# Fixed rounds over the experts, weights read where they stand, and a run-time rest

## The chip, the cores and the metric

The kernel runs on one core of one Trainium2 chip. The metric is the device time of one execution in microseconds (us), the median of several runs. TensorE (PE) multiplies, VectorE (DVE) and ScalarE (ACT) work element by element, GpSimd (POOL) issues the scatters, and SyncE (SP) issues loads, transposing DMAs and gathers. Each engine takes its own instructions in order.

## The reference

A gated linear scan over 4 sequences of 5056 tokens with 256 channels, then a mixture of 8 experts, where each of the 20224 tokens goes to the one expert with the largest logit:

```python
f = lower_bound + (1 - lower_bound) * sigmoid(f_logit); i = 1 - f
h = f[:, t] * h + i[:, t] * x[:, t]; y[:, t] = h          # for each t
logits = y @ w_gate; e_idx = argmax(logits)                # w_gate 256 x 8
gate_w = softmax(logits)[e_idx]; eom = sigmoid(y @ w_output_gate)
for e in range(8):                                         # w1 256 x 1024, w2 1024 x 256
    out[mask] = gate_w * eom[:, e] * (relu(y[mask] @ w1[e]) @ w2[e])
```

How many tokens an expert gets is known only when the kernel runs.

## The kernel before

**Chunks.** The scan and the gating run over 40 chunks of 512 tokens (`chunk`, L240). A chunk is a row of 17 stages, one per `yield` without a kind: stage 0 is a tanh on ACT (L251), 1 a product on DVE (L255), 3 the scan on DVE (L266), 5 a small matmul (L277), 6 a few small DVE instructions, 7 and 8 the high part (ACT, L296) and the low part (DVE, L300) of the rows, 10 the gating matmuls (L311, L316), 12 and 15 small DVE instructions, 16 four scatters (L413) of the rows to the region of their expert in `scr`. SP turns the rows by transposing DMAs in stages 8 and 10 (L293). In stage 4 a chunk issues the load of the next (L236, L237), into one of two buffers (`XB`).

**The order of the work.** `pump` runs one stage of each chunk under way beside the tasks of the experts; every `PERIOD` (8) pumps one more chunk begins. Up to a cut (the end of the weights' preparation) a scheduler orders the engines' instructions; behind it each engine takes them as the code makes them.

**Early tiles.** The weights are loaded and split into two float16 parts (`w1s`, `w2s`) in the first part of the run. Beside that, two rounds of 128 rows of each expert (`EARLY`, planned after chunks 3 and 5) are computed with the weights read where they stand (`first1`, `first2`).

**Run-time tiles.** All further work is done in tiles of 256 rows of one expert, which expert being a number that DVE computed (`plan`, some 24 small instructions for each two tiles) and that is loaded into a register (`expert`, L622). [...] `gemm1` (L655 to L657) makes four pieces `ph` of 2 x 256 columns, ACT takes the relu (L659), DVE its low part (`low`, L667), and `gemm2` (L685 to L687) follows one tile behind; then ACT scales (L728) and POOL scatters to the output (L732). There are 64 such tiles (`sure`: what any routing fills).

**The rest.** What is left is done in tiles of 128 rows, again with copies. Of these 18 are always run. Their true number, `count`, is loaded at the end, and two `tc.If` blocks (3 more tiles from 18, 16 more from 21) run where it is larger (L942 to L951).

Of the kernel before, what the change touches and what calls it, by code (L numbers as in the profile page):

```python
# [27 lines left out]
PERIOD = 8  # L28
PUMPS = 2.25
FILL = 12  # L30
MORE = (18, 21)
EARLY = (3, 5)
# [8 lines left out]
LEAD = 2  # L41
PLAN = 4
# [8 lines left out]
def tile_scan_moe(  # L51
# [32 lines left out]
    def sure(tokens):  # L84
        """tiles of 256 tokens of one expert that any routing of so many tokens fills beside the first tiles"""
        return max(0, -(-(tokens - len(EARLY) * E * P - E * 255) // 256))

# [7 lines left out]
    scr = dp.tile([E * R + P, RW], I16, name="scr")  # L95

# [16 lines left out]
    nc.gpsimd.iota(jcol, pattern=[[0, 1]], base=0, channel_multiplier=1, allow_small_or_imprecise_dtypes=True)  # L113
    eye = cp.tile([P, E], F32, name="eye")
# [19 lines left out]
    def pow2(ss, t, nm):  # L134
        """from a norm's square: s, a power of two with s times the norm below 2 ** t, and 2 / s"""
# [58 lines left out]
    # writes to rows of their own need no order among them; a reader waits for those it reads  # L194
# [12 lines left out]
    # rows behind each expert's rows: factor 0, an index no scatter takes  # L207
# [3 lines left out]
    fresh.append(nc.sync.dma_start(out=scr[FREE : FREE + P, :], in_=padt))  # L211
    apart(fresh[0], "scr")
    row2 = [cp.tile([P, NB, RW], I16, name=f"rows{i}") for i in range(2)]
    # the places of the last experts' weights serve the first chunks until then
# [25 lines left out]
    def chunk(c):  # L240
        """the steps of a chunk; each takes from the steps before what other engines made there"""
# [185 lines left out]
    firsts = []  # L427

    def plan_first():
        """for each expert: its next 128 rows, or the free rows behind all regions where it has fewer yet"""  # L430
# [8 lines left out]
        nc.vector.tensor_scalar(n, n, float(P), None, ALU.is_ge)  # L439
# [4 lines left out]
        nc.vector.scalar_tensor_tensor(out=dn, in0=n, scalar=float(P), in1=done, op0=ALU.mult, op1=ALU.add)  # L444
        yield SMALL
        nc.vector.scalar_tensor_tensor(out=m, in0=m, scalar=float(FREE), in1=eye, op0=ALU.add, op1=ALU.mult)
        tab = sp.tile([P, 2], I32, tag="pf_tab", name="pf_tab", bufs=len(EARLY))
# [6 lines left out]
        firsts.append([(tab, e, 1, new) for e in range(E)])  # L454

    def plan(k, nb, last):
# [27 lines left out]
        sel = t8("sel")  # L484
        yield SMALL
        nc.vector.tensor_scalar(sel, cum, jcol, None, ALU.is_gt)
        yield SMALL
        nc.vector.scalar_tensor_tensor(out=sel, in0=cex, scalar=jcol, in1=sel, op0=ALU.is_le, op1=ALU.mult)
        r = t8("r")
        yield SMALL  # L490
        nc.vector.tensor_scalar(r, cex, jcol, -float(unit), ALU.subtract, ALU.mult)
        yield SMALL
        nc.vector.scalar_tensor_tensor(out=r, in0=done, scalar=1.0, in1=r, op0=ALU.mult, op1=ALU.add)
        yield SMALL
        nc.vector.tensor_tensor(out=r, in0=r, in1=boff, op=ALU.add)
        yield SMALL
        nc.vector.tensor_tensor(out=r, in0=r, in1=sel, op=ALU.mult)
        if last:
            # slots past the last tile take the rows behind expert 0's
# [3 lines left out]
            idle = t8("idle")  # L503
            yield SMALL
            nc.vector.tensor_scalar(idle[:, 0:1], cum[:, E - 1 : E], jcol, cnt[:, 0:1], ALU.is_le, ALU.mult)
            yield SMALL
            nc.vector.tensor_tensor(out=r[:, 0:1], in0=r[:, 0:1], in1=idle[:, 0:1], op=ALU.add)
            prog["count"] = sp.tile([P, 1], I32, tag="pl_count", name="pl_count", bufs=1)
# [6 lines left out]
        tab = sp.tile([P, 2], I32, tag="pl_tab", name="pl_tab", bufs=8)  # L515
        new = list(fresh)
        fresh.clear()
        for j in range(k):
            slots.append((tab, j, nb, new))
        yield SMALL  # L520
        with nc.allow_low_precision("whole numbers"):
            nc.vector.tensor_reduce(out=tab[:, 0:1], in_=r, axis=AX.X, op=ALU.add)
        yield SMALL
        nc.vector.tensor_tensor(out=sel, in0=sel, in1=eidx, op=ALU.mult)
        yield SMALL
        with nc.allow_low_precision("whole numbers"):
            nc.vector.tensor_reduce(out=tab[:, 1:2], in_=sel, axis=AX.X, op=ALU.add)
# [74 lines left out]
    mpool = {}  # L602

    def gather(t, slot, e=None):
        tab, j, nb, new = slot
        n = nb * P
        r = nc.sync.value_load(tab[j : j + 1, 0:1], min_val=0, max_val=FREE + P - n)
        xq = gp.tile([P, 2, KD, 256], I16, tag="xq", name="xq")
        mt = gp.tile([P, 2, 4], I16, tag="mt", name="mt", bufs=4)
# [8 lines left out]
        return dict(xh=xq[:, 0].bitcast(F16), xl=xq[:, 1].bitcast(F16), mt=mt, nb=nb, tab=tab, j=j, id=t, ev=e)  # L618
# [5 lines left out]
    def factors(T):  # L624
        nb, ev = T["nb"], T["ev"]
        col = cinv[:, ev : ev + 1] if isinstance(ev, int) else cinv[:, ds(ev, 1)]
        fac = sp.tile([P, 2], F32, tag="fac", name="fac", bufs=4)
# [17 lines left out]

    def gemm1(T, q):
        mp, n = mpool["m"], T["nb"] * P
        ph = pp.tile([P, 2, 256], F32, tag="h", name="ph", bufs=4)
        w = T[f"w1_{q // 2}"]
        for i in range(2):  # L650
            f = (2 * q + i) % 4
            for k in range(KD):
                first, last = k == 0, k == KD - 1
                o = ph[:, i, 0:n]
                nc.tensor.matmul(out=o, lhsT=w[:, f, k, 0, :], rhs=T["xh"][:, k, 0:n], start=first, stop=False)  # L655
                nc.tensor.matmul(out=o, lhsT=w[:, f, k, 0, :], rhs=T["xl"][:, k, 0:n], start=False, stop=False)  # L656
                nc.tensor.matmul(out=o, lhsT=w[:, f, k, 1, :], rhs=T["xh"][:, k, 0:n], start=False, stop=last)  # L657
        hh = mp.tile([P, 2, 256], F16, tag="hh", name="hh", bufs=6)
        nc.scalar.activation(hh[:, :, 0:n], ph[:, :, 0:n], AF.Relu)  # L659
        T[f"h{q}"] = (ph, hh)  # L660

    def low(T, q):
        n = T["nb"] * P
        ph, hh = T[f"h{q}"]
        hl = mpool["m"].tile([P, 2, 256], F16, tag="hl", name="hl", bufs=6)
        yield BIG
        nc.vector.scalar_tensor_tensor(  # L667
            out=hl[:, :, 0:n], in0=ph[:, :, 0:n], scalar=0.0, in1=hh[:, :, 0:n], op0=ALU.max, op1=ALU.subtract
        )
        T[f"h{q}"] = (hh, hl)  # L670

    def gemm2(T, q):
        nb = T["nb"]
        if q == 0:
            T["y"] = pp.tile([P, 2, D], F32, tag="y", name="py", bufs=2)
        y, w = T["y"], T[f"w2_{q // 2}"]
        hh, hl = T.pop(f"h{q}")
        for i in range(2):
            f = (2 * q + i) % 4
            for b in range(nb):  # L680
                first = q == 0 and i == 0 and b == 0
                last = q == 3 and i == 1
                c = slice(b * P, (b + 1) * P)
                o = y[:, b, :]
                nc.tensor.matmul(out=o, lhsT=hh[:, i, c], rhs=w[:, f, 0, :], start=first, stop=False, skip_group_check=True)  # L685
                nc.tensor.matmul(out=o, lhsT=hh[:, i, c], rhs=w[:, f, 1, :], start=False, stop=False, skip_group_check=True)  # L686
                nc.tensor.matmul(out=o, lhsT=hl[:, i, c], rhs=w[:, f, 0, :], start=False, stop=last, skip_group_check=True)  # L687

    # the first tile of an expert: its weights are read where they stand
# [31 lines left out]
    def evacuate(T):  # L721
        nb = T["nb"]
        if isinstance(T["ev"], int):
# [15 lines left out]
    prog = {"begun": 0, "tick": 0, "done": 0, "left": 0.0, "planned": 0, "final": False, "got": 0, "rounds": 0}  # L739
    live = []  # L740
    total = sure(N)
    tail = (N - 256 * total + E * (P - 1)) // P
    ntile = total + tail

    planning = []

    def loading(c):
        """the steps of chunk c, with the load of the next once the chunk before has freed its place"""
# [241 lines left out]
```

## Time and profile before

| | |
|---|---|
| device time, 3 runs | 1030.67 us median, 1029.03 to 1031.43 |
| span of the profiled execution | 1016.9 us, which is 13.8 us below that median |
| PE, DVE, ACT, POOL busy | 911.9, 887.5, 511.4, 376.5 us |
| weight copies on DVE | 164 of `w1s` (115.1 us), 164 of `w2s` (111.8 us) |
| first run-time tile begins, last matmul | 183.2 us, 1000.26 us |

The page gives the profiled execution's span, from its first to its last instruction; its device time isn't listed apart, and the 13.8 us stand for what lies around the span. Busy time is the union of an engine's instructions. A busy PE is not PE at its peak, since matmuls are pipelined and overlap in the records: the start of one to the start of the next tells the rate.

### The profile page before, as it was taken

How to read it: one execution, taken by the hardware profiler on the slowest of the kernel's cores; microseconds unless marked ns; L12 is line 12 of the kernel's file. 1: busy time of each engine (PE TensorE's matmuls, PEld its weight loads, DVE VectorE, ACT ScalarE, POOL GpSimd, SP SyncE). 2: the span in 40 equal slices, each digit the busy share in tenths (PEclk: the TensorE clock that was granted, in tenths of full speed). 3: DMA queues.
4: the chain of work that ended last, by engine and by line, in shares of the span. 5: the costliest groups of instructions: out<-in, count | busy, mean ns of one | idle time of the engine just before them, and what ended most of it. 6: DMA issues, size and time to landing. Idle time of an engine off the chain costs nothing.

```text
span 1016.9 us, 27437 instructions
## 1 busy us (share of the span) xinstructions
PE 911.9 (90%) x9775; PEld 822.8 (81%) x9775; DVE 887.5 (87%) x2803; ACT 511.4 (50%) x1075; POOL 376.5 (37%) x378
## 2 busy tenths in 40 slices
PE   2268998899999999999999999999999999999993
PEld 2157887788888888888888888888888888899993
DVE  7989896899999999999999999999999998758781
ACT  5667774545545555455455554454455543333331
POOL 1523234343444444433444434344444344221221
PEclk9999999999999999999999999999999999999997
DMA  8899966755566565555565565555665534312120
GB/s 309 202 308 287 267 153 154 179 137 138 138 141 151 135 149 153 137 138 137 137 149 141 157 145 132 139 135 132 149 144 152 138 85 104 95 49 45 47 55 16
DMA packets 238547, 146.34 MB, mean 144 GB/s; under 512 B 202558, under 2 KB 204224, under 8 KB 238401
## 3 DMA queue, kind: packets, MB, share of 16 engines
q1 hardware_dynamic: 222752, 101.74, 43.2%
q0 software_dynamic: 15360, 42.74, 13.7%
q8 instruction: 80, 1.31, 0.6%
q14 instruction: 67, 0.54, 0.2%
q10 hardware_dynamic: 288, 0.02, 0.0%
HBM read 58.38 MB, written 44.49 MB: 101 GB/s over the span
## 4 chain that ended last, share of the span: by engine, by line
DVE 54%; issue 17%; DMA 11%; PE 10%; POOL 3%; ACT 2%; SPq 1%; DVEq 1%; POOLq 0%; ACTq 0%
DVE hl L667 11%; DVE xt L266 7%; DVE w L637 5%; DMA rows<-ft 5%; DVE w L643 4%; DVE xt L255 4%; DVE ft L300 3%; POOL out_dram L732 2%; PE ph L655 1%; PE ph L657 1%; PE ph L656 1%; DMA xq<-scr 1%; PE py L685 1%; PE py L687 1%; PE py L686 1%
## 5 line engine op out<-in xcount | busy, mean ns | idle before, releaser
L655 PE MATMUL ph<-xq,w 128*128 128x256 f16 (+1 forms) x1312 | 331.0, 261 | 0.3 <-DVE xv L142 0.3
L657 PE MATMUL ph<-xq,w 128*128 128x256 f16 (+1 forms) x1312 | 331.2, 261 | 0.0
L656 PE MATMUL ph<-xq,w 128*128 128x256 f16 (+1 forms) x1312 | 331.1, 261 | 0.0
L685 PE MATMUL py<-w,hh 128*128 128x256 f16 x1168 | 318.6, 273 | 0.5 <-ACT ft L296 0.3
L687 PE MATMUL py<-w,hl 128*128 128x256 f16 x1168 | 318.6, 273 | 0.0
L686 PE MATMUL py<-w,hh 128*128 128x256 f16 x1168 | 318.5, 273 | 0.0
L732 POOL DMA_INDIRECT out_dram<-yo,mt x146 | 167.9, 1150 | 298.8 <-ACT yo L728 275.1
L413 POOL DMA_INDIRECT scr<-rows,dst x154 | 175.4, 1139 | 229.3 <-issue 215.5
L659 ACT ACTIVATE hh<-ph 128x512 f16<-128x512 f32 (+1 forms) x328 | 178.7, 545 | 153.1 <-PE ph L657 152.8
L667 DVE SCALAR_TENSOR_TENSOR hl<-ph,hh 128x512 f16<-128x512 f32 (+1 forms) x328 | 204.6, 624 | 10.9 <-ACT hh L659 9.1
L655 PEld LDWEIGHTS <-w 128*128 128x128 f16 x1312 | 128.0, 98 | 12.4 <-DVE w L637 0.6
L637 DVE COPY w<-w1s 128x2048 f16 x164 | 115.1, 702 | 26.1 <-PE ph L657 24.7
L657 PEld LDWEIGHTS <-w 128*128 128x128 f16 x1312 | 128.1, 98 | 11.7
L656 PEld LDWEIGHTS <-w 128*128 128x128 f16 x1312 | 128.1, 98 | 11.4
L687 PEld LDWEIGHTS <-hl 128*128 128x128 f16 x1168 | 114.2, 98 | 13.2
L686 PEld LDWEIGHTS <-hh 128*128 128x128 f16 x1168 | 114.2, 98 | 13.2 <-issue 0.8
L685 PEld LDWEIGHTS <-hh 128*128 128x128 f16 x1168 | 114.2, 98 | 12.5
L643 DVE COPY w<-w2s 128x2048 f16 x164 | 111.8, 682 | 0.5 <-PE py L687 0.3
L260 ACT ACTIVATE ft<-ft,fb,fa 128x512 f32<-128x512 f32 (+1 forms) x76 | 60.6, 807 | 100.7 <-DVE xt L255 98.0
L296 ACT ACTIVATE ft<-xt,sa 128x512 f16<-128x512 f32 (+1 forms) x76 | 50.2, 708 | 106.1 <-DVE li L285 101.9
L266 DVE TENSOR_TENSOR_SCAN xt<-ft,xt 128x512 f32<-128x512 f32 (+4 forms) x78 | 90.7, 1170 | 0.0
L728 ACT ACTIVATE yo<-py,fac 128x256 f32<-128x256 f32 x146 | 61.6, 465 | 26.4 <-PE py L687 25.7
(178 smaller groups left out, 1311.5 us busy)
## 6 DMA issues: line engine op xcount, KB each, us to landing
ft<-in_fT_dram SPq DMA_DIRECT2D x37, 512.0 KB
xt<-in_xT_dram SPq DMA_DIRECT2D x37, 512.0 KB
w<-in_wT_dram SPq DMA_DIRECT2D x32, 512.0 KB
scr<-rows,dst POOLq DMA_INDIRECT x154, 3.3
rows<-ft SPq DMA_TRANSPOSE x152
out_dram<-yo,mt POOLq DMA_INDIRECT x146, 2.8
xq<-scr SPq DMA_TRANSPOSE x99
scr<-padt SPq DMA_DIRECT2D x9, 136.0 KB
```

Source lines behind the costliest of these rows:

```text
L266: nc.vector.tensor_tensor_scan(out=xt[:, k, a:z], data0=ft[:, k, a:z], data1=xt[:, k, a:z], initial=init, op0=ALU.mult, op1=ALU.add)
L413: ins = nc.gpsimd.indirect_dma_start(out=scr[:, :], out_offset=IOA(ap=dst[:, b : b + 1], axis=0), in_=rows[:, b, :], in_offset=None)
L637: nc.vector.tensor_copy(out=w, in_=w1f[:, ds(T["ev"] * (2 * WH) + h * 2 * QH, 2 * QH)])
L655: nc.tensor.matmul(out=o, lhsT=w[:, f, k, 0, :], rhs=T["xh"][:, k, 0:n], start=first, stop=False)
L656: nc.tensor.matmul(out=o, lhsT=w[:, f, k, 0, :], rhs=T["xl"][:, k, 0:n], start=False, stop=False)
L657: nc.tensor.matmul(out=o, lhsT=w[:, f, k, 1, :], rhs=T["xh"][:, k, 0:n], start=False, stop=last)
L659: nc.scalar.activation(hh[:, :, 0:n], ph[:, :, 0:n], AF.Relu)
L667: nc.vector.scalar_tensor_tensor(out=hl[:, :, 0:n], in0=ph[:, :, 0:n], scalar=0.0, in1=hh[:, :, 0:n], op0=ALU.max, op1=ALU.subtract)
L685: nc.tensor.matmul(out=o, lhsT=hh[:, i, c], rhs=w[:, f, 0, :], start=first, stop=False, skip_group_check=True)
L686: nc.tensor.matmul(out=o, lhsT=hh[:, i, c], rhs=w[:, f, 1, :], start=False, stop=False, skip_group_check=True)
L687: nc.tensor.matmul(out=o, lhsT=hl[:, i, c], rhs=w[:, f, 0, :], start=False, stop=last, skip_group_check=True)
L732: ins = nc.gpsimd.indirect_dma_start(out=out[:, :], out_offset=IOA(ap=T["mt"][:, b, 2:4].bitcast(I32), axis=0), in_=T["yo"][:, b, :], in_o ...
```

## The change

Eleven rounds with fixed experts take the place of the two early rounds and of most run-time tiles: six rounds of 128 rows of each expert and five of 256, each planned after a given chunk (`ROUNDS`). In a round every expert has its turn in fixed order, so the weights are read in place, without copies. An expert that does not yet have a full 128 or 256 rows when its round is planned gets a block of padding rows instead (`FREE`), and its rows stay for later (`plan_round`; the block is computed all the same). The first two rounds (`FIRST`) are computed early as before. What the fixed rounds leave is done with run-time tiles and copies: 8 tiles of 256 rows and then tiles of 128, of which again 18 are always run; if `count` is over 18, one block of 19 more is run, and within it, if it is over 37, one of 112 more. A chunk begins every 6 pumps instead of every 8. The work of the tiles is one row of pieces of 512 columns: a tile of 128 rows has two of them (before: four of 256), the second matmuls follow `LAG` (4) pieces behind, and the gathers are issued two tiles ahead instead of one.

```diff
-PERIOD = 8
+PERIOD = 6
-MORE = (18, 21)
-EARLY = (3, 5)
+MORE = (18, 37)
+ROUNDS = (
+    (1, 3), (1, 5), (1, 8), (1, 10), (1, 13), (1, 15),
+    (2, 19), (2, 23), (2, 28), (2, 33), (2, 37),
+)
+FIRST = 2
+LAG = 4
...
+    rows_round = sum(nb for nb, _ in ROUNDS) * P
+    total = max(0, -(-(N - E * rows_round - E * 255) // 256))
+    tail = (N - 256 * total + E * (P - 1)) // P
...
-        nc.vector.tensor_scalar(n, n, float(P), None, ALU.is_ge)
+        nc.vector.tensor_scalar(n, n, float(unit), None, ALU.is_ge)
...
+    def weights1(T, f):
+        return w1s[:, T["ev"], f] if T["fixed"] else T[f"w1_{f // 4}"][:, f % 4]
...
     def gemm1(T, q):
+        n, nf = T["nb"] * P, 4 // T["nb"]
+        ph = pp.tile([P, 512], F32, tag="h", name="ph", bufs=4)
+        for i in range(nf):
+            w, o = weights1(T, nf * q + i), piece(ph, T)[:, i, :]
...
+    fixed += [(r, e) for r in range(len(ROUNDS)) for e in range(turns[r] if r < FIRST else 0, E)]
+    ntile = len(fixed) + total + tail
...
+        for s in range(end + LAG + 2):
+            T, q = flat[s] if s < end else (None, 0)
+            U, u = flat[s - LAG] if LAG <= s < end + LAG else (None, 0)
+            if T is not None and q == 0 and T + 2 < t1 + more:
+                ahead(T + 2)
...
+            step(RATE, tasks)
...
+    base = len(fixed) + total
+    experts(0, base + cuts[0], 0)
...
+    def rest_of(i):
+        if i + 1 < len(cuts):
+            with tc.If(used > cuts[i]):
+                experts(base + cuts[i], base + cuts[i + 1], 0)
+                ordered(0, 0)
+                rest_of(i + 1)
```

On DVE, in the middle of the run. `hl` is the low part of a piece, `ft<-xt` (L300, now L307) and `xt<-ft` (L255, now L262; L266 the scan) are a chunk's, `w` the copied weights, `fac` the tile's factors. Before:

```order
L300 SCALAR_TENSOR_TENSOR ft<-xt,sa,ft 128x512
L629 ISA
L629 TENSOR_SCALAR fac<-mt,cinv 128x2
L255 SCALAR_TENSOR_TENSOR xt<-ft,xt 128x512
L643 ISA
L643 COPY w_0_8969<-w2s 128x2048
L667 SCALAR_TENSOR_TENSOR hl<-ph,hh 128x512
L255 SCALAR_TENSOR_TENSOR xt<-ft,xt 128x512
L637 ISA
L637 COPY w_1_9038<-w1s 128x2048
L667 SCALAR_TENSOR_TENSOR hl<-ph,hh 128x512
```

and now, at the same kind of place:

```order
L642 TENSOR_SCALAR fac<-mt,cinv 128x2
L262 SCALAR_TENSOR_TENSOR xt<-ft,xt 128x512
L687 SCALAR_TENSOR_TENSOR hl<-ph,hh 128x512
L262 SCALAR_TENSOR_TENSOR xt<-ft,xt 128x512
L307 SCALAR_TENSOR_TENSOR ft<-xt,sa,ft 128x512
L687 SCALAR_TENSOR_TENSOR hl<-ph,hh 128x512
L307 SCALAR_TENSOR_TENSOR ft<-xt,sa,ft 128x512
```

The copies are gone from between the low parts; two chunks' large instructions stand closer together.

On PE, at the end of what is always run, before (`L947` loads the count, `L949` is the branch):

```order
L687 LDWEIGHTS hl
L687 MATMUL py<-w_1_19982,hl 128x256
L947 TENSOR_LOAD pl_count
L949 COMPARE_AND_BRANCH
L655 LDWEIGHTS w_0_20034
L655 MATMUL ph<-xq,w_0_20034 128x128
```

and now (`L992` and `L986`):

```order
L704 LDWEIGHTS hl
L704 MATMUL py<-w_1_19072,hl 128x256
L992 TENSOR_LOAD pl_count
L986 COMPARE_AND_BRANCH
L676 LDWEIGHTS w_0_19174
L676 MATMUL ph<-xq,w_0_19174 128x128
```

The form is the same; what stands behind the first branch is now a block of 19 tiles (2736 instructions of PE, a load of weights and a matmul for each of 1368) instead of 3, and the second branch stands inside that block instead of behind it.

On SP, in the middle of the run, before, from a chunk's second pair of transposes (`rows<-ft`) to the next tile's gather (`xq`, `mt`):

```order
L293 DMA_TRANSPOSE rows_133<-ft 128x4x128 x2
L236 DMA ft<-in_fT_dram 128x2x512
L237 DMA xt<-in_xT_dram 128x2x512
L607 TENSOR_LOAD pl_tab
L607 ISA x2
L610 ISA
L610 DMA_TRANSPOSE xq<-scr 128x4x256
```

and now:

```order
L300 DMA_TRANSPOSE rows_136<-ft 128x4x128 x2
L243 DMA ft<-in_fT_dram 128x2x512
L244 DMA xt<-in_xT_dram 128x2x512
L620 TENSOR_LOAD tabs
L620 ISA x2
L623 ISA
L623 DMA_TRANSPOSE xq<-scr 128x4x128
```

The order is the same, but the next chunk begins two pumps after its load is issued, where it was four.

More of the change, by code (lines that the diff above doesn't have):

```diff
@@ L425, in tile_scan_moe, with plan_round @@
     slots = []
-    firsts = []
-    def plan_first():
+    rounds = []
+    tabs = cp.tile([P, 2 * len(ROUNDS)], I32, name="tabs")
+    def plan_round(nb):
+        unit = nb * P
         done = sched["done"]
@@ L453, in plan_first @@
         fresh.clear()
-        firsts.append([(tab, e, 1, new) for e in range(E)])
+        rounds.append([(tab, e, nb, new) for e in range(E)])
     def plan(k, nb, last):
@@ L502, in plan @@
             nc.vector.tensor_copy(out=ends, in_=cnt)
-            idle = t8("idle")
+            prog["count"] = sp.tile([P, 1], I32, tag="pl_count", name="pl_count", bufs=1)
             yield SMALL
[L505 to L508, printed above, removed]
             nc.vector.tensor_copy(out=prog["count"], in_=cum[:, E - 1 : E])
@@ L670, in low @@
         T[f"h{q}"] = (hh, hl)
     def gemm2(T, q):
-        nb = T["nb"]
+        nb, nf = T["nb"], 4 // T["nb"]
         if q == 0:
             T["y"] = pp.tile([P, 2, D], F32, tag="y", name="py", bufs=2)
[L676 to L679, printed above, removed]
-            for b in range(nb):
[L681 to L687, printed above, removed]
+        y = T["y"]
@@ L792, in step, with slot @@
             prog["left"] -= 1.0
-            pump(tasks, need)
+            pump(tasks)
             tasks = []
+    fixed = []
     tiles = {}
+    def slot(t):
+        if t < len(fixed):
+            r, e = fixed[t]
+            return (rounds[r][e], e) if r < len(rounds) else None
+        return (slots[t - len(fixed)], None) if t - len(fixed) < len(slots) else None
     def ahead(t):
-        while len(slots) <= t and len(slots) < ntile:
-            plans(1)
+        while not slot(t):
+            plans()
             if planning:
@@ L853, in tile_scan_moe @@
     deep = WPB // 2
-    for n in range(min(EARLY[0], NCH)):
+    for n in range(PRE):
         load_chunk(n)
@@ new lines, in experts, with later @@
+        nbs = [(2 if t - len(fixed) < total else 1) if t >= len(fixed) else ROUNDS[fixed[t][0]][0] for t in range(t0, t1)]
+        flat, begin, at = [], {}, {}
+        for t, nb in zip(range(t0, t1), nbs):
+            begin[t] = len(flat)
+            flat += [(t, q) for q in range(2 * nb)]
+        end = len(flat)
+        def later(s, act):
+            at.setdefault(s, []).append(act)
+        last = {}
+        for t, nb in zip(range(t0, t1), nbs):
+            if t < len(fixed):
+                continue
+            for fetch, h, lag in ((fetch1, 0, 0), (fetch1, 1, 0), (fetch2, 0, LAG), (fetch2, 1, LAG)):
+                use = begin[t] + h * nb + lag
+                s = last[fetch, h] + 1 if (fetch, h) in last else max(use - 2, 0)
+                assert s <= use
+                last[fetch, h] = use + nb - 1
+                later(s, (fetch, t, h))
@@ new lines, in experts @@
+        ahead(t0)
+        ahead(t0 + 1) if t0 + 1 < t1 else None
+        done = []
+        for s in range(end + LAG + 2):
+            tasks = []
+            T, q = flat[s] if s < end else (None, 0)
+            U, u = flat[s - LAG] if LAG <= s < end + LAG else (None, 0)
+            if T is not None and q == 0 and T + 2 < t1 + more:
+                ahead(T + 2)
+            for fetch, t, h in at.get(s, []):
+                X = tiles[t]
+                if X["ev"] is None:
+                    alone(expert(X))
+                tasks.append(fetch(X, h))
+            if U is not None and u == 0:
+                tasks.append(factors(tiles[U]))
+            if 1 <= s <= end:
+                t, p = flat[s - 1]
+                tasks.append(low(tiles[t], p))
+            step(RATE, tasks)
+            for X, age in done:
+                if age == s - 1:
+                    evacuate(X)
+                elif age == s - 2:
+                    put(X)
+            if T is not None:
+                gemm1(tiles[T], q)
+            if U is not None:
+                gemm2(tiles[U], u)
+                if u == 2 * tiles[U]["nb"] - 1:
+                    done.append((tiles[U], s))
```

225 lines of the change are left out of this document (95 added, 130 removed).

## The prediction, made before the changed kernel was run

> **What bounds the kernel now.** The first view is the page: who is busy, and what the weight copies cost.
>
> ```profile
> span 1016.9 us, 27437 instructions
> ...
> PE 911.9 (90%) x9775; PEld 822.8 (81%) x9775; DVE 887.5 (87%) x2803; ACT 511.4 (50%) x1075; POOL 376.5 (37%) x378
> ...
> L637 DVE COPY w<-w1s 128x2048 f16 x164 | 115.1, 702 | 26.1 <-PE ph L657 24.7
> ...
> L643 DVE COPY w<-w2s 128x2048 f16 x164 | 111.8, 682 | 0.5 <-PE py L687 0.3
> ```
>
> PE and DVE are level, so the page doesn't say who sets the pace. Two copies of each kind a tile make 82 tiles: 64 of 256 rows and 18 of 128. So neither closing block ran, and the count was at most 18. The second view is busy time by stretch (columns: stretch, its length, then PE, PEld, DVE, ACT, POOL).
>
> ```profile
> 0.00:50.00 50.00, 12.79 (x156) 10.43 (x157) 41.61 (x158) 31.65 (x61) 15.69 (x32) 1.00 0.88 257
> 50.00:100.00 50.00, 34.73 (x447) 31.65 (x447) 44.36 (x159) 34.11 (x58) 14.55 (x16) 0.97 1.04 292
> 100.00:150.00 50.00, 46.91 (x708) 44.24 (x705) 44.97 (x147) 37.34 (x64) 18.06 (x18) 1.00 0.90 224
> 150.00:200.00 50.00, 42.75 (x500) 38.54 (x501) 39.11 (x129) 25.98 (x56) 19.24 (x20) 0.97 0.71 152
> ...
> 400.00:500.00 100.00, 96.46 (x955) 86.34 (x953) 93.36 (x304) 50.03 (x111) 41.24 (x40) 1.00 0.56 145
> ...
> 850.00:900.00 50.00, 50.00 (x465) 44.82 (x463) 36.25 (x120) 14.96 (x30) 12.62 (x13) 1.00 0.29 81
> 900.00:950.00 50.00, 50.00 (x671) 47.29 (x668) 37.70 (x80) 18.50 (x47) 11.49 (x11) 1.00 0.21 47
> ```
>
> Up to 183 us, where the first run-time tile begins, DVE is the busy one (170.05 of 200 us) and the DMA engines are nearly full (the column ahead of the last: 0.88 to 1.04 up to 150 us). From there to the end PE is busy 96 to 100% at the full clock (the column behind POOL). How near it is to its own rate there is read from the starts of its matmuls, 12 of 256 columns and 12 of 128 columns in a row:
>
> ```profile
> 515.69 0.27 PE L655 MATMUL ph<-xq,w 128*128 128x256 f16 x1
> ...
> 516.89 0.27 PE L657 MATMUL ph<-xq,w 128*128 128x256 f16 x1
> ...
> 985.82 0.22 PE L655 MATMUL ph<-xq,w 128*128 128x128 f16 x1
> ...
> 986.44 0.22 PE L657 MATMUL ph<-xq,w 128*128 128x128 f16 x1
> ```
>
> 1.20 / 11 = 0.109 us with 256 columns and 0.62 / 11 = 0.056 with 128. A tile of 256 rows has 48 + 48 matmuls of 256 columns: 10.46 us. A tile of 128 has 48 of 128 columns and 24 of 256: 5.30 us, which is the interval of the closing tiles' scatters in the chain that ended last:
>
> ```profile
> 972.20 1.08 POOL out_dram L732
> ...
> 977.50 1.08 POOL out_dram L732
> ...
> 982.80 1.08 POOL out_dram L732
> ```
>
> So the closing tiles run at PE's own rate, copies and all. In the middle a tile takes longer; its 48 second matmuls are counted in a window of that tile's name alone, and the waits between 200 and 880 us say what is lost:
>
> ```profile
> 400.00:500.00 100.00, 51.91 (x424) 1.00 0.56 145
> ...
> PEld L316 <- DVE ft L300: 27.9, 28, 1.3
> PE pr L316 <- DVE ft L300: 25.3, 28, 1.2
> ```
>
> 424 / 48 = 8.83 tiles in 100 us, 11.32 us a tile or 22.6 a chunk. Above two tiles' 20.92 that leaves 1.7, of which 0.9 is PE waiting, once a chunk, for the low part of the rows from a DVE that is 93% busy; the rest is the chunk's own small matmuls, 0.8. The whole stretch therefore holds some 25 us that a free DVE could give back, not the 227 us of the copies.
>
> **The change part by part.** *Copies.* 64 tiles of 256 rows lose theirs, less the 8 that stay: 56 x 4 x 0.69 = 155 us of DVE. What DVE has to do then follows from these rows (forms apart: columns count | busy, mean ns):
>
> ```profile
> L667 DVE SCALAR_TENSOR_TENSOR hl<-ph,hh 128x512 f16<-128x512 f32 x256 | 174.3, 681 | 5.8 <-ACT hh L659 5.8
> ...
> L266 DVE TENSOR_TENSOR_SCAN xt<-ft,xt 128x512 f32<-128x512 f32 x64 | 81.2, 1271 | 0.0
> ...
> L300 DVE SCALAR_TENSOR_TENSOR ft<-xt,sa,ft 128x512 f16<-128x512 f32 x74 | 55.1, 749 | 18.8 <-DMA rows<-ft 13.4 <-ACT ft L251 3.8 <-ACT hh L659 1.0
> ...
> L255 DVE SCALAR_TENSOR_TENSOR xt<-ft,xt 128x512 f32<-128x512 f32 x74 | 50.9, 694 | 4.7 <-DMA xt<-in_xT_dram 3.7 <-ACT ft L251 1.1
> ...
> L346 DVE SCALAR_TENSOR_TENSOR key<-dl,rev 128x32 f32<-128x32 f32 x39 | 7.4, 190 | 1.1
> ```
>
> A chunk costs DVE 2 x (1.271 + 0.749 + 0.694) = 5.4 us and 24 small instructions of about 0.18, 9.7 in all. Six pumps then hold a chunk and six low parts of 0.681: 13.8 us, against 6 x 10.46 / 4 + 0.8 = 16.5 us of PE. DVE falls to 84% or less though chunks come faster. Of the 25 us of waiting I take 20 as gained; the bounds are 28 (all of it, by the longer of the two rows) and 0 (the wait moves to another hand-over).
>
> *The early part.* With a chunk every 6 pumps, 11 chunks are done when the first later tile begins (pump 74 by the code's own counting) where it was 9 (pump 77). Two chunks are 19.4 us of DVE, less the first `plan` (24 small instructions, 4 us): 15. DVE was idle for 30 of the 200 us there, so between 0 (they fit) and 20 (they don't, and their loads, 2 MB, queue behind the weights as well). DVE at 85% is nearer to full: +12. Later the two chunks' small matmuls are missing: -1.
>
> *Smaller tiles.* Sixteen tiles of 256 become 32 of 128: 32 x 5.30 - 16 x 10.46 = +2. Reading weights in place costs PE nothing: the copies had the same layout. ACT and DVE handle the same 512 columns an instruction.
>
> *POOL and SP.* Scatters per row are unchanged. SP gains 16 gathers and is moved past nothing, but has them in less room; every fixed round is planned at least four tiles before its first gather, so no tile waits for its plan.
>
> *The closing block.* This is the largest term. Which tokens go where follows from the reference's inputs; I counted them with its formulas. The experts get 2482, 2625, 2388, 2599, 2384, 2354, 2539 and 2853 tokens. For the kernel before, the same counting gives a rest of exactly 18 tiles, as the 82 tiles above demand. For the changed one: when the round of 256 after chunk 23 is planned, expert 1 has 236 rows not yet taken; 20 short, it gets padding, and its 256 rows stay for later. All other turns are full (the next nearest have 135 of 128 and 299 of 256). After the rounds 434, 833, 340, 551, 336, 306, 491 and 805 rows are left; the eight tiles of 256 go to experts 0 to 4 (1, 3, 1, 2, 1); the others leave 178, 65, 84, 39, 80, 306, 491 and 805, in tiles of 128: 2 + 1 + 1 + 1 + 1 + 3 + 4 + 7 = 20. That is over 18, so the block of 19 tiles runs, 2 of them with rows and 17 with none. A tile without rows costs PE the same: 19 x 5.30 = +101 us, behind everything else and covered by nothing.
>
> Entering it is not in the trace; what stands at the branches is:
>
> ```profile
> L949 SPq COMPARE_BRANCH  x2: 50/52/53, 991.2 to 991.9; - x2
> ...
> L949 PEldq COMPARE_BRANCH  x2: 4232/4514/4796, 999.4 to 1003.9; - x2
> ...
> L947 PEldq TENSOR_LOAD <-pl_count x1: 483/483/483, 998.8 to 998.8; - x1
> ```
>
> PE loads the count (0.5 us), then waits for the first two copies (1.4 us). In the first four steps only first matmuls run, 24 x 0.056 = 1.3 us each, while DVE has a copy or two and a low part, about 2.1: 4 x 0.8 = 3. Together +5; the bounds are 0.5 (all prepared during PE's last tile) and 12 (with a branch of PE's long kind and what that delays). At the end one skipped block of PE's two is left, so nothing is added there.
>
> [...] The trace's branches that skip a block took PE 4.2 and 4.8 us, and SP 0.05. [...]
>
> *The sum*: +101 + 5 + 2 - 20 + 12 - 1 = +99. The profiled span becomes 1016.9 + 99 = 1116; on the median of the runs, which is 13.8 above that span, 1030.67 + 99 = 1130.
>
> **Rivals.** *The block isn't entered.* The count would have to be 18 or less, two tiles fewer than I count, as it would be if expert 1 had 20 more rows by chunk 23. Then the other terms stand alone: 1030.67 + 2 - 20 + 11 = 1024, faster, and with all waits gone 1016. For it speaks that before the block was not entered; against it the count, with 20 rows of margin, and that eleven other draws of the same generator leave 20 to 24.
>
> *All that DVE gives up reaches the end.* Early chunks fit into the idle 30 us, the waits vanish, the block is entered smoothly: 101 + 1 + 2 - 28 - 1 = +75, 1106. For it: PE's own rate in the closing tiles. Against: full DMA engines early.
>
> *Chunk loads come late.* These are one chunk's load on SP and the tanh that uses it on ACT:
>
> ```profile
> 512.67 0.39 SPq L236 DMA_DIRECT2D ft<-in_fT_dram  x1
> 514.82 0.38 SPq L237 DMA_DIRECT2D xt<-in_xT_dram  x1
> ...
> 525.91 1.14 ACT L251 ACTIVATE ft<-ft 128x512 f32<-128x512 f32 x2
> ```
>
> 13.2 us lie between. The load now has two pumps less, 5.2 us: 8 are left, and 1 MB at the 145 GB/s of that stretch takes 7. ACT takes the tanh in order, with the relus behind it. If each of the 29 later chunks held PE up by 2.5 us, that is +73, so 1203; it decides once a tanh is later than the four pieces between first and second matmuls (`LAG`) can take up. Against it: the transposes that free the buffer also come earlier when DVE isn't behind.
>
> **How the numbers follow.** My case (block entered, some waits left) has 0.72 and lies between 1112 and 1150; all gains arrive, 0.13, around 1106; late loads, 0.10, 1150 to 1205; block not entered, 0.05, 1016 to 1026. The range of 8 in 10 is 1104 to 1158: the lower end is the second case, the upper adds the worse ends of the early part (+8), the entry (+7) and part of the waits (+13). A difference under 0.2% (2 us) is no change for this measurement: faster 0.05, same 0.01, slower 0.94.
>
> **What would show it.** In the profile after, the copies count 2 x (26 + 19) = 90 of each kind, not 52, and the scatters behind the always-run part keep an interval of 5.30 us for 19 tiles with no chunk left. In the middle the wait of PE for the low part of the rows is mostly gone, DVE is below 85%, and a tile of 256 takes under 11.1 us. The first later tile begins at 185 to 200 us. I am wrong if the copies count 52 each; if PE shows new waits for a chunk's load; or if the closing tiles are slower than 5.4 us each.

## The result: 1219 us, slower by 18%, and the profile after

The changed kernel takes 1218.99 us (median of 4 runs, 1209.38 to 1224.33), the kernel before 1031.05 beside it: a ratio of 1.1813, 95% interval 1.1753 to 1.1872. The forecast was 1130 and had the sign; it missed 89 of the 188 us that were lost. The profiled run took 1222.72 us with a span of 1221.0, so 1.7 us lie around a span and not 13.8: the profile of before simply came from a faster execution (1016.9 + 1.7), which matters below.

The page of the changed kernel, its first lines and the groups of the copies:

```profile
span 1221.0 us, 31293 instructions
...
PE 1060.3 (87%) x11911; PEld 947.9 (78%) x11911; DVE 742.9 (61%) x2177; ACT 541.0 (44%) x1096; POOL 366.9 (30%) x398
...
L656 DVE COPY w<-w2s 128x2048 f16 x90 | 63.1, 701 | 87.1 <-PE py L704 87.0
L650 DVE COPY w<-w1s 128x2048 f16 x90 | 62.3, 693 | 3.5 <-PE ph L678 2.4 <-issue 1.1
```

The copies count 90 of each kind, so the block of 19 tiles ran. Busy time by stretch (columns as in the prediction):

```profile
50.00:100.00 50.00, 22.29 (x254) 19.72 (x254) 39.16 (x149) 29.56 (x51) 14.02 (x16) 0.67 0.84 229
100.00:150.00 50.00, 39.81 (x542) 37.30 (x540) 37.92 (x122) 29.26 (x52) 14.66 (x15) 0.90 0.98 229
...
300.00:400.00 100.00, 86.81 (x1072) 77.31 (x1071) 55.56 (x193) 46.36 (x99) 32.87 (x38) 0.90 0.56 141
...
600.00:700.00 100.00, 91.89 (x904) 78.76 (x903) 64.53 (x216) 53.11 (x118) 36.52 (x41) 0.98 0.64 152
...
800.00:900.00 100.00, 100.00 (x919) 89.64 (x917) 28.87 (x51) 31.27 (x59) 19.67 (x20) 1.00 0.24 61
```

Three things are to be seen. In the early part PE is busy for less of the time than before (22.3 of 50 us where it was 34.7), and from 100 to 150 us at a lower clock (0.90 where it was 1.00; ahead of 67.1 us the trace of before has no record of the clock, so its 1.00 and 0.97 there can't be compared). The first later tile begins at 228.7 us, not 183.2. In the middle DVE is free (56 to 65%), as forecast, yet PE is busy 87 to 92% where it was 96, at 0.90 to 0.98 of its clock. Behind 800 us, with no chunk left, PE runs at its own rate. The end is the forecast block; the chain that ended last has its scatters:

```profile
1123.44 1.35 POOL out_dram L749
1124.80 3.66 issue
1128.69 1.40 POOL out_dram L749
1130.10 3.71 issue
1134.04 1.35 POOL out_dram L749
```

5.25 to 5.35 us apart. What PE loses in the middle is in no list of waits for another engine; it stands in the timeline (start, length, then in brackets the idle time before it):

```profile
366.50 0.22 PE L677 MATMUL ph<-xq,w1s 128*128 128x128 f16 x1
367.35 0.22 PE L678 MATMUL ph<-xq,w1s 128*128 128x128 f16 x1 [0.63 <-issue]
367.40 0.22 PE L676 MATMUL ph<-xq,w1s 128*128 128x128 f16 x1
368.08 0.22 PE L677 MATMUL ph<-xq,w1s 128*128 128x128 f16 x1 [0.46 <-issue]
368.80 0.23 PE L678 MATMUL ph<-xq,w1s 128*128 128x128 f16 x1 [0.50 <-issue]
368.86 0.27 PE L702 MATMUL py<-w2s,hh 128*128 128x256 f16 x1
368.97 0.28 PE L703 MATMUL py<-w2s,hh 128*128 128x256 f16 x1
370.21 0.37 PE L704 MATMUL py<-w2s,hl 128*128 128x256 f16 x1 [0.96 <-issue]
370.38 0.42 PE L702 MATMUL py<-w2s,hh 128*128 128x256 f16 x1
370.59 0.42 PE L703 MATMUL py<-w2s,hh 128*128 128x256 f16 x1
```

In the middle of one tile's matmuls, which wait for nothing ("issue"), PE advances for 3.7 us by one or two instructions per 0.7 us, and then runs at half speed (0.21 us from start to start, 0.109 before). I call this a stall. In the trace of before there is none behind 190 us; here nearly every chunk has one. Up to 460 us it begins 3.4 to 4.5 us behind the first of the chunk's four scatters (L420), later mostly 6 to 7 us behind it; most are within 7 us of a load, but the last two, at 760 and 775 us, come 24 and 39 us behind the last load. No load of instructions falls into the one shown: in the trace's list of packets neither of the two instruction queues (q8 and q14 of the page) has one under way between 360.4 and 372.1 us. The theories at first: (1) the rhythm of 6 pumps brings scatters, transposes and load of different chunks together, and their transfers starve PE; (2) PE reads weights in place that the transfers disturb; (3) tiles of 128 rows need twice the instructions per us.

### The profile page after: what moved, and what is told of

Same layout as the page of the kernel before. It is cut to its first block, busy times and chain, and to the rows that moved or that the text cites. A ratio compares the mean times of both kernels' runs of the same rounds, so it can differ in the third digit from the quotient of the medians.

```text
span 1221.0 us, 31293 instructions
## 1 busy us (share of the span) xinstructions
PE 1060.3 (87%) x11911; PEld 947.9 (78%) x11911; DVE 742.9 (61%) x2177; ACT 541.0 (44%) x1096; POOL 366.9 (30%) x398
## 4 chain that ended last, share of the span: by engine, by line
PE 45%; issue 32%; DVE 7%; POOL 6%; DMA 6%; SPq 2%; ACT 1%; POOLq 0%; another core or an unknown queue 0%; DVEq 0%; ACTq 0%
PE ph L676 7%; PE ph L677 7%; PE ph L678 7%; PE py L703 7%; PE py L704 7%; PE py L702 7%; POOL out_dram L749 6%; DMA mt<-scr 1%; DMA rows<-ft 1%; DMA ft<-in_fT_dram 1%; DMA xq<-scr 1%; DVE xt L273 1%; DMA w<-in_wT_dram 1%; DVE ft L307 1%; DVE w1s L612 1%
## 5 line engine op out<-in xcount | busy, mean ns | idle before, releaser
L680 ACT ACTIVATE hh<-ph 128x512 f16<-128x512 f32 x330 | 196.7, 597 | 473.9 <-PE ph L678 320.8
L687 DVE SCALAR_TENSOR_TENSOR hl<-ph,hh 128x512 f16<-128x512 f32 x330 | 226.7, 688 | 278.9 <-ACT hh L680 181.3
L676 PE MATMUL ph<-xq,w1s 128*128 128x256 f16 (+1 forms) x1152 | 273.9, 255 | 14.3 <-issue 7.4
L677 PE MATMUL ph<-xq,w1s 128*128 128x256 f16 (+1 forms) x1152 | 274.1, 255 | 12.4 <-issue 12.2
L678 PE MATMUL ph<-xq,w1s 128*128 128x256 f16 (+1 forms) x1152 | 274.2, 255 | 7.4 <-issue 7.4
L703 PE MATMUL py<-w2s,hh 128*128 128x256 f16 x896 | 249.8, 279 | 11.9 <-issue 11.8
L704 PE MATMUL py<-w2s,hl 128*128 128x256 f16 x896 | 249.9, 279 | 9.7 <-issue 9.5
L702 PE MATMUL py<-w2s,hh 128*128 128x256 f16 x896 | 249.8, 279 | 6.4 <-issue 6.3
L420 POOL DMA_INDIRECT scr<-rows,dst x154 | 153.9, 999 | 278.6 <-issue 257.2
L676 PE MATMUL ph<-xq,w 128*128 128x128 f16 (+1 forms) x720 | 137.8, 229 | 0.5 <-DVE w L650 0.5
L677 PE MATMUL ph<-xq,w 128*128 128x128 f16 (+1 forms) x720 | 137.8, 229 | 0.0
L678 PE MATMUL ph<-xq,w 128*128 128x128 f16 (+1 forms) x720 | 137.8, 229 | 0.0
L677 PEld LDWEIGHTS <-w1s 128*128 128x128 f16 x1152 | 116.0, 101 | 26.6 <-issue 18.6
L678 PEld LDWEIGHTS <-w1s 128*128 128x128 f16 x1152 | 116.1, 101 | 23.3 <-issue 15.3
L676 PEld LDWEIGHTS <-w1s 128*128 128x128 f16 x1152 | 115.9, 101 | 17.7 <-issue 9.7
L656 DVE COPY w<-w2s 128x2048 f16 x90 | 63.1, 701 | 87.1 <-PE py L704 87.0
L704 PE MATMUL py<-w,hl 128*128 128x256 f16 x424 | 115.6, 273 | 0.0
L703 PE MATMUL py<-w,hh 128*128 128x256 f16 x424 | 115.6, 273 | 0.0
```

Of the source, the lines that this page charges most:

```text
L420: ins = nc.gpsimd.indirect_dma_start(out=scr[:, :], out_offset=IOA(ap=dst[:, b : b + 1], axis=0), in_=rows[:, b, :], in_offset=None)
L656: nc.vector.tensor_copy(out=w, in_=w2f[:, ds(T["ev"] * (2 * WH) + h * 2 * QH, 2 * QH)])
L676: nc.tensor.matmul(out=o, lhsT=w[:, k, 0, :], rhs=x, start=(k == 0), stop=False)
L677: nc.tensor.matmul(out=o, lhsT=w[:, k, 0, :], rhs=y, start=False, stop=False)
L678: nc.tensor.matmul(out=o, lhsT=w[:, k, 1, :], rhs=x, start=False, stop=(k == KD - 1))
L680: nc.scalar.activation(hh, ph, AF.Relu)
```

## The experiments

"Set" means kernels run one after the other on one chip, with the kernel before among them. It took 1029.1, 1030.2 and 1027.0 us in three sets (e1 to e4, e5 to e8, f1 to f4) and 1020.7 and 1021.6 in two (e9 to e11, f5 to f7). That turned out to matter. The differences of e1 to e8 are to the 1218.99 above; the changed kernel took 1221.36 when it was run again (f1).

**e1, the block.** `MORE = (20, 37)`.

> The changed kernel with the first cut of the rest at 20 tiles instead of 18, so that the block of 19 tiles is skipped; the two tiles of it that hold rows are now in the part that always runs. If the block costs what the chain of the changed kernel shows (19 scatter intervals of 5.30 us, 101 us, and an entry of some us), the time falls from 1219 to about 1219 - 101 + 2 x 5.3 = 1128 us. If part of the block were hidden or were paid for something else (the skip of a longer block, the last scatters), the fall would be under 70 us.

1140.24 us, ratio 1.1091 (1.105 to 1.1131): 79 less, 12 short of what was expected, and no run says where the 12 are. The block is the largest single loss. A price without the two extra tiles comes with f2.

**e2, scatters later.**

```diff
+        for _ in range(2 if c >= 9 else 0):
+            yield
         for b in range(nb):
             ins = nc.gpsimd.indirect_dma_start(out=scr[:, :], ...
```

> The changed kernel with two more empty stages ahead of a chunk's scatters, from chunk 9 on, so that they no longer fall into the pump in which the next chunk's second transposes and the load after next are issued. In the profile of the changed kernel PE stalls for 2 to 4 us once per chunk, in the middle of its matmuls and with no semaphore in the way, each time beginning at the third or fourth scatter of a chunk, and runs at half clock for some us behind that. Theory 1 (the transfers of one chunk piled on each other starve PE): the stalls shrink to under 1.5 us a chunk, and the time falls by 40 to 70 us to 1150 to 1180. Theory 2 (PE reads the weights in place, from a region that the transfers disturb) and theory 3 (tiles of 128 rows ask for twice the instructions): no change within 12 us. If the scatters alone do it, the stalls move two pumps later at the same size.

1184.17 us, ratio 1.1519 (1.1445 to 1.1593): 35 less, under the 40 to 70 that theory 1 asked for and over the 12 of the others. PE's busy share rises:

```profile
600.00:700.00 100.00, 95.15 (x962) 83.67 (x962) 70.08 (x230) 59.01 (x130) 40.52 (x44) 1.00 0.68 166
```

But the edit did not part what it was meant to part. In its trace, up to 450 us, the scatters still stand between transposes and a load (first scatter at 390.57 us, transposes issued 1.9 and 0.0 us ahead of it, a load 3.2 behind; in the changed kernel at 385.29: 2.3, 0.6 and 1.9), and the stalls still begin 3.4 to 4.9 us behind the first scatter. So the gain is real, and theory 1 is not tested by it.

**e3, larger tiles.** `(1, 8), (1, 10), (1, 13), (1, 15)` become `(2, 10), (2, 15)`.

> The changed kernel with the four later rounds of 128 rows made into two rounds of 256 (after chunks 10 and 15), so that PE gets half as many instructions per us for the tiles between 229 and 480 us. Theory 3 (the instruction rate of small tiles makes the stalls): the loss above PE's own rate there falls from 22 us to the 12 us per 100 us seen behind 500 us, about 25 us less in all, so about 1194. Theories 1 and 2: the same stalls, 1219 within 8 us (32 x 5.30 against 16 x 10.46 is 2 us).

1194.54 us, ratio 1.1608 (1.1571 to 1.1645): 24 less, as theory 3 had it. The stalls are somewhat shorter with large tiles but don't go: small tiles add to them and are not needed for them.

**e4, copied weights for the fixed rounds too.** `weights1` and `weights2` return the copies for every tile, and `fetch1`, `fetch2`, which make these copies on DVE, are issued for the fixed ones too.

> The changed kernel with the fixed rounds after the first two computed from copies of their weights, as the run-time tiles are: 72 x 4 more copies of about 0.69 us on DVE, 199 us. Theory 2 (reading in place makes the stalls): they vanish, and the loss of 11 to 25 us per 100 us between 229 and 776 us falls to about 5, that is 50 to 70 us less, unless DVE, now near 95% busy, takes part of it back: 1150 to 1190. Theories 1 and 3: the stalls stay, and with DVE's copies on top the time is 1219 to 1260.

1223.78 us, ratio 1.191 (1.184 to 1.1981): 5 more. Between 300 and 400 us PE is busy 84.1% (86.8 in the changed kernel), with the same kind of stalls, though it reads copies. So reading in place is not needed for a stall. That the time is the same doesn't mean that the copies change nothing, though. The idle time of PE that the list of waits puts down to "issue" falls from 26.4 to 22.8 us between 230 and 445 us, and from 28.4 to 12.4 between 445 and 790; against it stand new waits for the copies, between 230 and 445 us:

```profile
PE ph L680 <- DVE w L654: 17.2, 16, 7.6
```

Whether the copies themselves or the changed spacing of the work lessen the late stalls is not shown.

**e5, a chunk every 7 pumps.** `PERIOD = 7`.

> The changed kernel with a chunk every 7 pumps. A chunk's scatters then share a pump with no second transposes and no load: these are issued one and two pumps later. Five pumps have to be run without a tile, because a round is wanted before its chunk is done (some 3 us each). Theory 1 (scatters that meet a chunk's other transfers make the stalls): the stalls behind 229 us nearly vanish, 40 to 60 us less; with some 10 us less in the early part and 15 more for the empty pumps about 1165 (1145 to 1185). Theory 3 alone (the instruction rate of small tiles): stalls as before, 1210 to 1230.

1161.42 us, ratio 1.1274 (1.1233 to 1.1314): 58 less. The first later tile begins 20.6 us earlier (208.1), and the stalls become rarer, though between 250 and 400 us most stay. There the load isn't what begins them: the first of a chunk's scatters at 302.0 us, for one, has its stall 8.0 us behind it and the next load 10.0 us behind it.

**e6, before, with later scatters.** Four stages by the edit of e2, `c >= 10`.

> The kernel before (tiles of 256 rows, copied weights, a chunk every 8 pumps) with four empty stages ahead of the scatters of every chunk from chunk 10 on, so that they fall into the pump in which a later chunk's load is issued. Theory 1: stalls of 2 to 3 us per chunk appear in the middle of PE's matmuls, also with copied weights and large tiles: 28 x 2 to 3.5 us, so 1085 to 1130. Theories 2 and 3 (in-place weights or small tiles are needed for it): no change, 1025 to 1036.

1026.52 us, ratio 0.9961 (0.9938 to 0.9984). Behind 190 us PE has three single gaps of up to 1.1 us put down to "issue" (3.1 us in all), and nothing like a stall per chunk. This run does not test what it was meant to: in its trace three of a chunk's four scatters stand as far ahead of the load as before (7.4 to 4.4 us), and only the fourth moved, to 2.4 us behind it. It is of use otherwise: it is the one trace with 8 pumps from a set in which e5, e7 and e8 stall, and its first run-time tile begins at 192.7 us, its last matmul 816.0 us later (183.2 and 817.1 in the profile of before). So what the kernel before loses in such a set seems to lie in the early part.

**e7, the early part.** `GAPS = (3, 3) + (8,) * 8`.

> The changed kernel with a chunk every 8 pumps for the first ten chunks and every 6 after that: three chunks fewer before the run-time part. If the early 45 us are lost to chunks that are packed too closely while the weights are prepared, the first later tile begins at 183 to 190 us instead of 229, and the time falls by 35 to 45 us less three chunks' matmuls, to 1175 to 1188. If it is the form of the work there that costs (order of pieces, the plans), under 10 us.

1177.53 us, ratio 1.1451 (1.1393 to 1.1508): 41 less. The first later tile begins at 196.3 us, close to the 192.7 of e6 in the same set. Most of the early loss is that of the rhythm.

**e8, before, with a chunk every 6 pumps.** `PERIOD = 6`.

> The kernel before with a chunk every 6 pumps and nothing else. Two chunks more in the early part: if packing is what costs there, the first run-time tile begins 35 to 45 us later. In the middle VectorE would need 17.9 us per chunk (9.7 for the chunk, 6 x 0.68 low parts, 6 copies of 0.69) where PE needs 16.5, so PE waits 1.4 us or more a chunk, 40 us, and theory 1 adds stalls where scatters meet transposes and loads: 1030 + 40 + 40 + 0 to 60, 1100 to 1170. If neither holds, 1030 to 1060.

1083.75 us, ratio 1.0556 (1.0499 to 1.0613): 53.6 more, between the two ranges expected (1100 to 1170, 1030 to 1060). The first run-time tile begins at 218.1 us, 35 later than in the profile of before and 25 later than in e6, which is of the same set. And stalls stand in the middle, with copied weights and tiles of 256:

```profile
512.01 0.27 PE L656 MATMUL ph<-xq,w 128*128 128x256 f16 x1
512.19 0.27 PE L657 MATMUL ph<-xq,w 128*128 128x256 f16 x1
512.91 0.27 PE L655 MATMUL ph<-xq,w 128*128 128x256 f16 x1 [0.46 <-issue]
513.62 0.27 PE L656 MATMUL ph<-xq,w 128*128 128x256 f16 x1 [0.43 <-issue]
514.33 0.27 PE L657 MATMUL ph<-xq,w 128*128 128x256 f16 x1 [0.44 <-issue]
515.07 0.27 PE L655 MATMUL ph<-xq,w 128*128 128x256 f16 x1 [0.47 <-issue]
```

One matmul per 0.72 us. So neither small tiles nor weights in place are needed for a stall; of all that the diff changes, the period alone is enough to bring it.

**e9, before, with smaller matmuls.** Each first matmul of 256 columns becomes two of 128.

> The kernel before with the first matmuls of its tiles of 256 rows split into two of 128 columns each: the same rhythm of 8 pumps, the same transfers and copies, and the same PE time by the closing tiles (2 x 0.056 us against 0.109), but 144 matmuls a tile instead of 96, the rate of the changed kernel's small tiles. Theory 3 (the instruction rate alone makes the stalls): stalls of 2 us or more per chunk appear in the middle, 28 x 2 to 4 us, 1085 to 1140. Theory 1 (the rhythm of 6, in which transfers meet, is needed): no stalls, 1030 to 1042.

1023.32 us against 1020.69, ratio 1.0027 (1.0006 to 1.0048), no stalls. But in this set no kernel stalled, so it says nothing on theory 3; it shows that half the columns at twice the count cost 2.6 us in all.

**e10, the missed turn.** `(2, 23)` becomes `(2, 24)`.

> The changed kernel with the second round of 256 planned after chunk 24 instead of 23. Expert 1 then has its 256 rows, no turn is filled with padding, and the rest is counted at 18 tiles, so the block must not run though its cut stays at 18. If the one missed turn is what starts the block: 1219 - 101 - 0 to 5 = 1113 to 1125, or, since skipping at 20 tiles brought 79 and two tiles more go, some 1130. If the count were over 18 for another reason: 1219 as before.

1070.46 us, ratio 1.0485 (1.0433 to 1.0537): far below every expectation. The block is gone, and so are the stalls, from the first chunk on, although up to chunk 23 the instructions are the changed kernel's own.

**e11, three edits together.** `(2, 24)`, `PERIOD = 7`, and `(2, 10)` for `(1, 8), (1, 10)`.

> Four of the edits together: the round after chunk 24 (no block), a chunk every 7 pumps (-58 alone), one pair of rounds of 128 as a round of 256 after chunk 10 (half of an edit that brought 25). Six pumps run without a tile. If the parts add up: 1219 - 90 - 58 - 10 = 1061 (1045 to 1075), still behind the kernel before. If period and tile size take the same stalls away twice: 1070 to 1080.

1046.26 us, ratio 1.0214 (1.0158 to 1.0269), also in the set without stalls, so that the agreement with the expected 1061 (1045 to 1075), which was summed from runs with stalls, is luck. Whether the stalls belong to the kernel or to the set was open now, so the changed kernel was run again beside three others.

**f1 to f4, in one set.** No new edits: the changed kernel, e10, e5 and e8 again.

> The changed kernel unchanged, in a set of runs with the three others. If the stalls belong to the place and time: in a set where the kernel before takes about 1020 us there are none, and it takes some 1165 to 1175 (the 1070 of e10 and the block's 95 to 105); in a set where the kernel before takes 1030 they are there, and it takes about 1219. If they belong to the kernel: 1219 in both.

> The round after chunk 24 again, beside the changed kernel. Whatever the set, the difference to the changed kernel is the block alone, 95 to 105 us, and the profile up to chunk 23 has the same stalls or none in both. If the missed turn made the stalls: 1070 here beside 1219.

> A chunk every 7 pumps, beside the changed kernel. With stalls in the set: 58 us less than the changed kernel, as before. Without: the early part (20 us less) less the five empty pumps (15 us more): within 15 us of the changed kernel.

> The kernel before with a chunk every 6 pumps, beside the changed kernel. With stalls in the set: 53 us over the kernel before, as in e8. Without: the early 35 us and VectorE's 1.4 us a chunk, part of which the wait for low parts already held: 30 to 50 us over.

1221.36, 1123.26, 1164.17 and 1082.46 us, with the kernel before at 1027.04 (ratios 1.1894 (1.185 to 1.1937), 1.0959 (1.0904 to 1.1014), 1.1352 (1.1306 to 1.1398), 1.0534 (1.0482 to 1.0586)). e5 and e8 repeat, 57 less than the changed kernel and 55 more than the kernel before. The difference of the first two is the block: 98.1 us. And the kernel of e10, 1070.46 in its own set, takes 1123.26 here. Its stretches in this set, and then in that of e10:

```profile
500.00:600.00 100.00, 91.89 (x923) 79.79 (x921) 65.83 (x219) 54.05 (x121) 38.25 (x43) 1.00 0.64 157
600.00:700.00 100.00, 91.31 (x907) 79.04 (x905) 62.89 (x205) 52.71 (x115) 39.44 (x45) 1.00 0.68 161
```

```profile
500.00:600.00 100.00, 98.90 (x1012) 88.83 (x1011) 72.38 (x236) 60.34 (x133) 42.70 (x48) 1.00 0.73 177
600.00:700.00 100.00, 98.13 (x1004) 88.14 (x1002) 72.06 (x247) 60.18 (x136) 43.96 (x48) 1.00 0.75 173
```

So one and the same kernel stalls in one set and not in another, for 53 us. It isn't the chip: the chip of e1 to e4 (stalls) is that of e9 to e11 (none), and that of f1 to f4 is that of f5 to f7 (none). What differs between the sets stays open. What no run shows either is which part of the chip holds PE up. That scatters, transposes and a load meet is not enough: in e10 they stand as close (first scatter at 370.09 us, transposes 1.7 and 0.4 us ahead, a load 2.7 behind), and PE runs through. And every execution on record is a profiled one, so nothing shows whether the stalls are there without the profiler.

**f5 to f7, what the parts leave.** f5: `(2, 24)` and the `GAPS` of e7. f6: f5 with the later scatters of e2. f7: f5 with `(2, 10)` for `(1, 8), (1, 10)`.

> The changed kernel with the round after chunk 24 (the block is not entered, 98 us) and a chunk every 8 pumps for the first ten chunks (41 us in e7): both undone at once. If the parts add up: in a set without stalls (the kernel before at 1020) 1070 - 41 = 1029, within 1.5% of the kernel before; in a set with stalls (before at 1028) 1123 - 41 = 1082.

> The same with two more empty stages ahead of a chunk's scatters from chunk 9 on (35 us in e2). In a set with stalls: 1082 - 20 to 35, 1047 to 1062. In a set without: no stall is there to be shortened, 1025 to 1035.

> The first of these with one pair of rounds of 128 as one round of 256 (after chunk 10): half the gathers and fewer PE instructions there, one pump without a tile more or less. Half of the 25 us of e3 in a set with stalls: 1070. In a set without, some of the waits for gathered rows of small tiles go (16 us in e10): 1020 to 1028, so level with the kernel before.

1059.31, 1063.09 and 1046.06 us beside 1021.55 (ratios 1.0382 (1.0338 to 1.0425), 1.0391 (1.0345 to 1.0437), 1.025 (1.0218 to 1.0282)), without stalls. Later scatters bring nothing where there is no stall, which fits the 35 us of e2 being shorter stalls. All three missed what was expected of a set without stalls (1029, 1025 to 1035, 1020 to 1028). In f5 the first later tile came 32 us earlier than in e10 (193.9 against 225.7), the last matmul only 11 (1041.4 against 1052.8). The rest went to waits: those that the lists name for PE in the middle sum to 49.8 us in f5 and to 30.7 in e10. The largest of f5, between 194 and 720 us, and the wait of ACT that makes it (in the trace the tanh, L258, stands directly ahead of the evacuation, L745, which empties a tile's sums `py` into `yo`, in all 11 cases, after a wait of 6.4 to 10.5 us):

```profile
ACT ft L258 <- DMA ft<-in_fT_dram: 148.7, 27, 10.5
...
PE py L702 <- ACT yo L745: 29.0, 11, 4.6
```

One instance, on SP, ACT and PE:

```profile
332.46 2.94 SPq L300 DMA_TRANSPOSE rows<-ft  x2
337.94 0.40 SPq L243 DMA_DIRECT2D ft<-in_fT_dram  x1
...
341.78 1.15 ACT L258 ACTIVATE ft<-ft 128x512 f32<-128x512 f32 x2 [9.14 <-DMA ft<-in_fT_dram]
342.84 0.46 ACT L745 ACTIVATE yo<-py,fac 128x256 f32<-128x256 f32 x1
...
343.34 0.27 PE L702 MATMUL py<-w2s,hh 128*128 128x256 f16 x1 [3.26 <-ACT yo L745]
```

The load is issued 5.5 us behind the start of the transposes that free its buffer. The tanh stands at the head of ACT's queue for 9 us; behind it the evacuation of the last tile, and PE can't begin the next sums before that. This is the third rival of the prediction, late chunk loads, and it is there once the stalls no longer stretch the chunks. No version beats the kernel before.

## Why the prediction was wrong, step by step

In terms measured in sets of one kind (the profile of before, 1018.6 us with its 1.7, is by its time of the kind without stalls, as e10):

| term | predicted | measured | from |
|---|---|---|---|
| block and its entry | +106 | +98 | f1 - f2 |
| early part | +12 (0 to 20) | +42.5 | first later tile, e10 225.7, before 183.2 |
| middle: waits, smaller tiles, -1 | -19 | +10 | e10 225.7 to 1052.8, before 183.2 to 1000.3 |
| stalls | none | about +46 | e10 in two sets, 52.8, less the kernel before's own 6.4 (from its first later tile at 227.4 us to its last matmul at 1101.1, f2 takes 46.6 longer than e10) |
| sum | +99 | +197 by parts | f1 less the kernel before in its set: 194.3 |

*The block: right.* The count was over 18, since the block ran, and not over 20, since e1 skipped it at a cut of 20; and it came from the one missed turn: e10 gives the expert those rows, and the block goes. The entry was the part sized too high, +5: in the trace of the changed kernel PE passes from the last matmul ahead of the block to the first in it without a pause (1110.87 and 1110.98 us) and waits 0.17 and 0.29 us for copies behind that, which is the lower bound. The whole block holds PE from 1110.98 to 1212.4, 101.4 us; the 98 of f1 and f2 is a difference of medians, and the runs of f2 alone spread over 10.6. The branches:

```profile
L986 PEldq COMPARE_BRANCH  x3: 92/193/3469, 1110.0 to 1214.6; - x3
```

Falling through into the block took PE 0.09 us, skipping the nested one 3.5; the third, behind it, took 0.19. The +5 has nothing in it for the first of these: that falling through is free was the author's assumption, since the trace of before has no branch of PE that falls through, and the 0.09 us came close to it.

*The early part: that two more chunks would crowd it was right; what they crowd and the size were not.* The step that failed is "between 0 (they fit) and 20 (they don't)": it sized the crowding by DVE's time, and DVE was no busier than before (39 of 50 us). PE waited, for the gathers of its early tiles; before, and after:

```profile
PE ph L697 <- DMA xq<-scr: 12.8, 7, 3.7
```

```profile
PEld L715 <- issue: 29.6, 9, 10.9
PE ph L714 <- DMA xq<-scr: 29.0, 7, 10.9
```

The DMA engines were no fuller than before (0.84 to 0.98 up to 150 us; before 0.88 to 1.04). e7 and f5 show that the rhythm is most of the cause: with the first ten chunks 8 pumps apart, f5 begins its first later tile at 193.9 us and waits 10.9 us for the early gathers. That gives back 31.8 of the 42.5 us; what the other 10.7 are, and how the loss divides between SP's order and the transfers, was not taken apart.

*The middle: the gain came, and new waits ate it.* The wait for the low part is gone (0.7 us in e10, 25.3 before), DVE is at 72% against the 84% at most, and from 500 to 600 us of e10 a tile of 256 takes 100 x 48 / 442 = 10.9 us, under the 11.1 named. That reading weights in place costs PE nothing held at PE's own rate: ahead of the stall shown, matmuls that read `w1s` in place start 0.056 us apart (365.83 to 366.50 us), as those with copies do in the closing tiles of the kernel before. The step that failed is "20 as gained": its other bound, "the wait moves to another hand-over", was named and then discounted. In e10 between 226 and 720 us:

```profile
PE pv L284 <- ACT ft L280: 13.5, 16, 1.3
PE ph L676 <- DMA xq<-scr: 13.0, 6, 3.5
...
PE pr L323 <- DVE ft L307: 0.7, 3, 0.3
...
ACT ft L258 <- DMA ft<-in_fT_dram: 127.4, 25, 10.5
```

The square (L280) stands on ACT, in order with a tanh that waits up to 10.5 us for its load; the gathers of `xq` are issued on SP right behind that load. The rival of late loads was given 0.10 by the argument that the transposes come earlier too; SP's row above shows that they don't come early enough. In f5 its price is 29 us of PE.

*The stalls: not in the prediction.* Nothing in the profile of before shows one, and it could not: that profile is from an execution without them. One sign was there and was read wrongly, the 13.8 us between its span and the median, which I put down to what lies around a span. Apart from 1.7 us it was mostly the difference between two kinds of sets. Shown is that a chunk every 6 pumps brings stalls to either kernel in some sets, where a chunk every 8 shows next to none (e6); that large tiles (e3), later scatters (e2) and a period of 7 (e5) lessen them; and that neither small tiles nor weights in place are needed (e8), though with copies the stalls behind 445 us are fewer (e4). Which resource holds PE up was not shown, so the cause of this term stays open.

## What to carry to other kernels

A change of rhythm is a change to every in-order queue, not only to the engine that was busiest: for each queue, ask which transfer now comes right before the instruction that waits for it, and what is queued behind. A block that runs only above a count is best priced by counting the real data; here one missed turn of 20 rows cost 98 us. And when a profile's span and the median of the runs differ by as much as here (13.8 us, 1.3%, where 1.7 us is what lies around a span), find out whether they are two kinds of execution before any term is sized by it.

## What was unexpected in the hardware

- PE stalled in the middle of matmuls that wait for no semaphore, one or two instructions per 0.72 us for 2 to 4 us, in some sets of runs and not in others on the same chip; the two sets differ by 53 us of 1123 in one kernel, of which the kernel before shows 6 as well.
- The stall shown goes together with a lower clock. The trace's clock record grants half from 369.1 to 375.9 us, beginning 2.6 us into a stall in which PE was never idle for over 1 us at a time. Behind the stall, matmuls of 256 columns start 0.21 us apart (370.38 to 372.30 us), and those of 128 columns 0.107 apart (up to 374.86); at the full clock the traces have 0.109 (before, 515.69 to 516.89 us) and 0.056 (in the changed kernel, 365.83 to 366.50 us). What brings the halving was not shown.
- The branch that PE fell through took 0.09 us, the one with which it skipped a block 3.5 (4.2 and 4.8 in the kernel before).
